# Finer loads of the first batch, a third input buffer and a reordered start in a Fourier-mixing and channel-mix kernel

## The chip, the cores and the metric

The kernel runs on one core of one Trainium2 chip. The metric is the device time of one execution in microseconds (us), and the number given is the median of ten executions.

A core has five engines that run their own instruction streams. The profile calls them PE (TensorE, matrix products), DVE (VectorE), ACT (ScalarE), POOL (GpSimd) and SP (SyncE, which here only issues transfers). PEld is the loading of a matrix into PE. Transfers between the chip's main memory (HBM) and the core's own memory (SBUF) are done by 16 DMA engines. They are issued from a queue of POOL, SP or ACT, and tell by a semaphore when they have landed. Matrix products go to a small memory called PSUM, from where ACT or DVE must "evacuate" them to SBUF.

## The reference

`x` has 8 batches of 3,072 rows of 256 numbers. First comes a two-dimensional Fourier transform of each batch, of which the real part is kept. Then comes a channel mix with a gate:

```python
X = np.fft.fft(np.fft.fft(x, axis=1), axis=2).real

x_prev = X shifted down by one row, zeros in the first row
xk = mu_k * X + (1.0 - mu_k) * x_prev
xr = mu_r * X + (1.0 - mu_r) * x_prev
k = np.maximum(xk @ w_k, 0.0)              # 256 -> 1024
v = k * k @ w_v                            # 1024 -> 256
out = v / (1.0 + np.exp(-(xr @ w_r)))      # w_r: 256 -> 256
```

## The kernel before

**The transform as matrix products.** The 3,072 rows are split into 96 partitions of 32 rows each. Stage A multiplies by a small matrix over the 96 partitions (`w_pm`), stage D transforms along the 256 columns (`w_eo`), and stage C finishes the transform along the rows with `m1` and `m2`, which hold sines of a table of angles. DVE then forms sums, differences (`halves`, `diff`) and the mixed inputs (`mix_part`, `mix`) for the channel mix.

**The channel mix.** For each of 48 chunks of 512 rows, four steps (`k_piece`) make the 1,024 hidden channels (L589), evacuated by ACT with Relu (L599); DVE squares them (L606), PE multiplies by `wv_sb` (L627), and DVE multiplies by the gate and writes the output tile (L637), which SP sends to memory. The transform of later batches is threaded between these steps by hand: `at(step, f, ...)` lists what is done at which step. At the end `pin_order` fixes the order of the instructions on each engine to the one in which they were written.

**Loads of x.** The loads convert from 32-bit to 16-bit numbers and are issued from POOL by `load_part(b, h, q0, nq)` (L102): half `h` (16 rows for each partition) of batch `b`, `nq` rows from `q0`. A half lives in a tile of the pool `xh`, which has two buffers (L58). The loads that concern us are:

- batch 0, half 0, in two parts of eight rows (L167, L172), and half 1 in four parts of four rows (L184 to L190);
- batch 1, half 0, in two parts of eight rows, and half 1 in one piece, in `loads()` (L372), between the weights: gathers of `wk` and `wr` by row numbers that POOL computes just before (`rows`, L287), and `wv`;
- later halves by `load_xh` (L107) at steps of the loop. A load into a buffer waits until the readers of the half that it held are done. For batch 0 and one half of batch 1 the reader is PE (`a_sum`, L444); for the others it is DVE (`butterfly`, L113), which writes even and odd sums that `a_item` then uses.

**The start.** Between the loads of batch 0, POOL makes counters with IOTA (`pcol_i`, `k1c_i`, `veo_i`, `kst_i`) and two small tables (`pd_f`, `ueo`). After the last load it makes `unit`, a 2 x 2 unit matrix (L191), with which `mu_turn` (L158) turns the rows of `mu_k` and `mu_r` into columns on PE. DVE and ACT make `w_pm`, `w_eo` and the angle tables meanwhile. `keep_busy` (L136) issues PE work on zeros.

**Stage A of batch 0.** `a_sum(b, h, q0, eng, n)` makes the products of `n` rows and evacuates them on the engine named (`"A"` for ACT, `"V"` for DVE). With `n` = 4 it takes one of three PSUM slots in turn (`ps_w`), with `n` = 2 one of two (`ps_v`). The order from L649 on is the one that the change edits. Into it are put the sine of the first 17 slices of angles (`m_sine(0, NS1)`, on ACT, NS1 = 17), `m_swap`, `m_zero`, and the second angles, slices 17 to 27, in two pieces (`m_angles(NS1, 22)` and `m_angles(22, NSL)`, on DVE, NSL = 27). After it come `mu_turn`, stage D in halves (`d_half`), stage C (`c_item`), and the first hidden products.

Of the kernel before, what the change touches and what calls it, by code (L numbers as in the profile page):

```python
# [13 lines left out]
AF = mybir.ActivationFunctionType  # L14
ALU = mybir.AluOpType
# [5 lines left out]
def _v(ap, extra_offset, free_dims):  # L21
    new_ap = [list(ap.ap[0])] + [[s, c] for (s, c) in free_dims]
    return dataclasses.replace(ap, offset=ap.offset + extra_offset, ap=new_ap)
# [12 lines left out]
def kernel(  # L36
# [10 lines left out]
    nc = tc.nc  # L47
# [5 lines left out]
    NSL = 27  # L53
    GU = 386
    NS1 = 17

    const = ctx.enter_context(tc.tile_pool(name="const", bufs=1))
    xh_pool = ctx.enter_context(tc.tile_pool(name="xh", bufs=2))  # L58
    eo_pool = ctx.enter_context(tc.tile_pool(name="eo", bufs=2))
    y_pool = ctx.enter_context(tc.tile_pool(name="y_sb", bufs=1))  # L60
    mix_pool = ctx.enter_context(tc.tile_pool(name="mix", bufs=1))
# [12 lines left out]
    def ps_w():  # L74
        return ps_slot("W", 3, 1024)

    def ps_v():
        return ps_slot("V", 2, 512)
# [23 lines left out]
    def load_part(b, h, q0, nq):  # L102

        nc.gpsimd.dma_start(out=xh_t[b, h][:, q0:q0 + nq],  # L104
                            in_=x_r[b, :, 16 * h + q0:16 * h + q0 + nq, :])
# [5 lines left out]
    V = nc.vector  # L111
# [24 lines left out]
    def keep_busy(n):  # L136

        ps = ps_v()
        for _ in range(n):
            nc.tensor.matmul(out=ps[:, 0:512], lhsT=zeros, rhs=_v(zeros, 0, [(0, 4), (1, P)]),  # L140
                             start=True, stop=True)
# [6 lines left out]
    unit = const.tile([2, 2], FP32)  # L148
# [3 lines left out]
    def mu_rows(a):  # L152
        for p0, f0, step, n in (((0, 0, 1, 1), (1, 1, 2, 64), (65, 2, 2, 63)),
                                ((0, 128, 1, 1), (1, 255, -2, 64), (65, 254, -2, 63)))[a]:
            nc.scalar.activation(out=mu_p[:, a, p0:p0 + n], in_=_v(mu_row, f0, [(step, n)]),
                                 func=AF.Copy)
# [7 lines left out]

    for h in range(2):
        xh_t[0, h] = xh_pool.tile([96, 16, 256], FP16, name="xh")
    load_part(0, 0, 0, 8)  # L167
    pcol_i = const.tile([P, 1], INT32)
    nc.gpsimd.iota(pcol_i, pattern=[[0, 1]], base=0, channel_multiplier=1)
    k1c_i = const.tile([P, 24, 2], INT32)  # L170
    nc.gpsimd.iota(k1c_i, pattern=[[1, 24], [0, 2]], base=0, channel_multiplier=0)
    load_part(0, 0, 8, 8)  # L172
    veo_i = const.tile([P, 2, 64], INT32)
    nc.gpsimd.iota(veo_i, pattern=[[-1, 2], [2, 64]], base=2, channel_multiplier=0)

# [4 lines left out]
                            op0=ALU.mult)  # L180
    for c in range(2):
        nc.gpsimd.tensor_scalar(out=ueo[:, :, c], in0=veo_i, scalar1=pd_f,
                                scalar2=(0.5 + 0.25 * c) * TURN, op0=ALU.mult, op1=ALU.add)
    load_part(0, 1, 0, 4)  # L184
    load_part(0, 1, 4, 4)
    kst_i = const.tile([P, NSL + 64], INT32)
    nc.gpsimd.iota(kst_i[:, 0:NSL], pattern=[[1, NSL]], base=-1, channel_multiplier=0)
    nc.gpsimd.iota(kst_i[:, NSL:NSL + 64], pattern=[[1, 64]], base=0, channel_multiplier=0)
    load_part(0, 1, 8, 4)
    load_part(0, 1, 12, 4)  # L190
    for i in range(2):  # L191
        nc.gpsimd.tensor_scalar(out=unit[:, i:i + 1], in0=pcol_i[0:2], scalar1=float(i),
                                scalar2=None, op0=ALU.is_equal)

    m_pi = const.tile([P, 1], FP32)
    V.memset(m_pi, -math.pi)
# [3 lines left out]
    def phase(lo, hi):  # L200
        lo, hi = (lo + 0.5) % 1.0, (hi + 0.5) % 1.0
        if (lo, hi) not in phs:
            t = const.tile([P, 1], FP32, name=f"ph{len(phs)}")
            V.memset(t[0:64], lo * TURN)
            V.memset(t[64:128], hi * TURN)
            phs[lo, hi] = t
        return phs[lo, hi]
# [12 lines left out]
    for c0, c1 in ((258, GU), (257, 258), (0, 1)):  # L220
        nc.scalar.activation(out=g_all[:, 13:NU, c0:c1],
                             in_=_v(zeros, 0, [(0, NU - 13), (1, c1 - c0)]), func=AF.Copy)
    mu_rows(0)

    pcol_f = const.tile([P, 1], FP32)
# [17 lines left out]
                    op0=ALU.mult, op1=ALU.add)  # L243
# [3 lines left out]
                    scalar2=0.5 / N1, op0=ALU.mult, op1=ALU.mult)  # L247
    V.tensor_tensor(out=u48, in0=u48, in1=ph48.rearrange("p a b -> p (a b)"), op=ALU.add)
    V.tensor_scalar(out=r48, in0=u48, scalar1=MAGIC, scalar2=MAGIC,
                    op0=ALU.add, op1=ALU.subtract)  # L250
    V.tensor_tensor(out=u48, in0=u48, in1=r48, op=ALU.subtract)
    nc.scalar.activation(out=t48, in_=u48, func=AF.Sin, bias=0.0, scale=TWO_PI)
    mu_rows(1)

    for g in range(2):
        for n in range(2):
            V.tensor_scalar(out=w_sg[:, n, g:g + 1], in0=g_i, scalar1=2.0 * g - 1.0,
                            scalar2=1.0 - g, op0=ALU.mult, op1=ALU.add)
        V.tensor_scalar(out=w_sg[:, 2, g:g + 1], in0=g_i, scalar1=1.0 - 2.0 * g,
                        scalar2=g - 1.0, op0=ALU.mult, op1=ALU.add)  # L260
# [5 lines left out]
                    op0=ALU.bitwise_and, op1=ALU.logical_shift_right)  # L266
# [4 lines left out]
                    op0=ALU.bitwise_and, op1=ALU.logical_shift_left)  # L271
# [7 lines left out]
                    scalar2=float(TURN) / R, op0=ALU.mult, op1=ALU.mult)  # L279
# [3 lines left out]
                    scalar2=phase(0.25, 0.0), op0=ALU.mult, op1=ALU.add)  # L283
# [33 lines left out]
    def m_angles(s0, s1):  # L317
        V.tensor_tensor(out=ang[:, s0:s1], in0=_v(ast, s0, [(1, s1 - s0), (0, 64)]),
                        in1=_v(ast, NSL, [(0, s1 - s0), (1, 64)]), op=ALU.add)
# [5 lines left out]
    def m_sine(s0, s1):  # L325
        nc.scalar.activation(out=m1[:, s0:s1], in_=ang[:, s0:s1], func=AF.Sin, bias=m_pi,
                             scale=TWO_PI / TURN)
# [3 lines left out]
    def m_swap(s0, s1):  # L331

        V.tensor_scalar(out=m2[lo64, s0:s1], in0=m1[hi64, s0:s1], scalar1=-1.0, scalar2=None,
                        op0=ALU.mult)
        V.tensor_copy(out=m2[hi64, s0:s1], in_=m1[lo64, s0:s1])
        if s0 == 0:
            for m in (m1, m2):
                V.memset(m[:, 0, 0:1], 0.0)

    def m_ends():  # L340


        for m in (m1, m2):
            nc.scalar.activation(out=m[hi64, 0], in_=m[hi64, 0], func=AF.Copy, scale=-1.0)

    def m_zero():
        for n, m in enumerate((m1, m2)):
            nc.scalar.activation(out=mz[lo64, n], in_=m[lo64, 1], func=AF.Copy)
# [73 lines left out]
    def evac(out_ap, in_ap, eng):  # L422
        if eng == "V":
            V.tensor_copy(out=out_ap, in_=in_ap)  # L424
        else:
            nc.scalar.activation(out=out_ap, in_=in_ap, func=AF.Copy)  # L426

    def a_tile(b):
        a_t[b] = y_pool.tile([P, 2, 48, 64], FP16, name="a")
# [13 lines left out]
    def a_sum(b, h, q0, eng="A", n=4):  # L443


        if (h, q0) == (0, 0):
            a_tile(b)
        xh = xh_t[b, h]
        ps = ps_w() if n == 4 else ps_v()
        for i in range(n):  # L450
            for k in range(2):
                nc.tensor.matmul(out=ps[:, 256 * i:256 * i + 192],  # L452
                                 lhsT=xh[:, q0 + i, 128 * k:128 * k + 128],
                                 rhs=w_pm[0:96, k:k + 2], start=(k == 0), stop=(k == 1))
        evac(_v(a_t[b], 2 * (16 * h + q0), [(64, 96), (2, n), (1, 2)]),
             _v(ps, 0, [(2, 96), (256, n), (1, 2)]), eng)
# [195 lines left out]
    a_sum(0, 0, 0)  # L652
    a_sum(0, 0, 4)
    keep_busy(1)
    m_sine(0, NS1)
    a_sum(0, 0, 8, "V")
    a_sum(0, 0, 12)
    m_angles(NS1, 22)
    m_swap(0, NS1)
    a_sum(0, 1, 0, "V")  # L660
    a_sum(0, 1, 4)
    m_zero()
    a_sum(0, 1, 8)
    a_sum(0, 1, 12, "V", 2)
    a_sum(0, 1, 14, "A", 2)
    m_angles(22, NSL)
    m_ends()
    mu_turn()
    d_half(0, 0, ps_v(), "A")
# [172 lines left out]
```

## Time and profile before

| what | us |
|---|---|
| median of ten executions | 455.89 (455.17 to 459.57) |
| the profiled execution | 456.39 |
| its span, first to last instruction | 454.6 |
| PE busy | 444.4 (98%) |
| ACT busy | 361.7 (80%) |
| DVE busy | 356.1 (78%) |
| POOL busy | 37.7 (8%) |

The span is what one execution's trace covers; some 1.8 us of the profiled execution lie around it. "Busy" sums the instructions of an engine. An engine may be busy all the time in one stage and idle in another, so the stages are looked at one by one. POOL works almost only in the first 45 us. Its transfers of x are these (issuing engine, number, size of each in 32-bit bytes, and the median time from issue to landing):

```profile
xh<-in_x_dram POOLq DMA_DIRECT2D x13, 768.0 KB, 6.9
xh<-in_x_dram POOLq DMA_DIRECT2D x4, 384.0 KB, 6.7
xh<-in_x_dram POOLq DMA_DIRECT2D x4, 192.0 KB, 6.3
```

The order of POOL's work at the start, with the start and the length of each group in us, is:

```profile
1.26 0.66 POOL L104 DMA_DIRECT2D xh<-in_x_dram  x1 [0.81 <-POOLq L826]
2.02 0.16 POOL L169 IOTA pcol_i<- 128x1 int32 x1
2.12 0.27 POOL L171 IOTA k1c_i<- 128x48 int32 x1
2.32 0.56 POOL L104 DMA_DIRECT2D xh<-in_x_dram  x1
2.88 0.27 POOL L174 IOTA veo_i<- 128x128 int32 x1
3.23 0.24 POOL L179 TENSOR_SCALAR pd_f<-pcol_i 128x1 f32<-128x1 int32 x1
3.57 0.77 POOL L182 TENSOR_SCALAR ueo<-veo_i,pd_f 128x128 int32<-128x128 int32 x2
4.30 1.06 POOL L104 DMA_DIRECT2D xh<-in_x_dram  x2
5.36 0.19 POOL L187 IOTA kst_i<- 128x27 int32 x1
5.47 0.22 POOL L188 IOTA kst_i<- 128x64 int32 x1
5.60 1.03 POOL L104 DMA_DIRECT2D xh<-in_x_dram  x2
6.64 1.40 POOL L192 TENSOR_SCALAR unit<-pcol_i 2x1 f32<-2x1 int32 x2
10.88 0.56 POOL L104 DMA_DIRECT2D xh<-in_x_dram  x1 [2.85 <-PE psW L452]
```

The bracket at the end of a line gives idle time of the engine before it and what ended it. The load at 10.88 is the first one of batch 1.

### The profile page before, as it was taken

The page shows a single profiled execution, that of the slowest core. Times are in us where ns is not written, and L with a number is a line of the kernel's source. Part 1 is how long each engine was busy: PE and PEld are TensorE (multiplying, and loading weights), DVE is VectorE, ACT ScalarE, POOL GpSimd, SP SyncE. Part 2 cuts the span into 40 slices and gives each one's busy share as a digit, 9 for nine tenths or more (in the row PEclk, how much of TensorE's full clock was granted, in tenths as well). Part 3 has the DMA queues.
Part 4 walks back from the last instruction along what each step waited for, and adds up shares of the span by engine and source line. Part 5 has one row for each costly group of instructions (what it writes and reads, how often), then busy time and mean ns, then how long its engine had stood idle before and what let it go on. Part 6 is the DMA issues. An engine that isn't in the chain of part 4 may idle for free.

```text
span 454.6 us, 9755 instructions
## 1 busy us (share of the span) xinstructions
PE 444.4 (98%) x4082; PEld 326.6 (72%) x4082; DVE 356.1 (78%) x495; ACT 361.7 (80%) x413; POOL 37.7 (8%) x72
## 2 busy tenths in 40 slices
PE   7899999999999999999999999999999999999995
PEld 4667777777777777777777777777777777666764
DVE  7899879977797869877789877987779755997453
ACT  7899997888788888788877888788878888666661
POOL 6848000000000000000000000000000000000000
PEclk9999999999999999999999999999999999999999
DMA  7775862627422473226622256221222122222223
GB/s 137 117 142 94 186 140 48 139 54 147 104 71 49 92 159 75 52 67 125 130 58 61 70 118 135 52 71 48 71 48 71 48 69 49 70 70 71 71 69 94
DMA packets 32524, 40.25 MB, mean 89 GB/s; under 512 B 3838, under 2 KB 29952, under 8 KB 31232
## 3 DMA queue, kind: packets, MB, share of 16 engines
q1 hardware_dynamic: 27776, 25.07, 22.0%
q0 software_dynamic: 4544, 14.42, 18.6%
q8 instruction: 32, 0.52, 0.5%
q10 hardware_dynamic: 160, 0.13, 0.1%
q14 instruction: 12, 0.10, 0.1%
HBM read 28.84 MB, written 25.17 MB: 119 GB/s over the span
## 4 chain that ended last, share of the span: by engine, by line
PE 93%; ACT 3%; DMA 1%; POOL 1%; issue 1%; DVE 0%; POOLq 0%
PE psV L627 37%; PE psW L589 35%; PE psW L613 9%; PE psW L462 4%; PE psW L438 4%; PE psW L493 3%; DMA xh<-in_x_dram 1%; ACT rl L599 1%; ACT g_all L426 1%; POOL xh L104 1%; PE psW L452 0%; DVE g_all L424 0%; ACT L618 0%; ACT pq L426 0%; ACT r L618 0%
## 5 line engine op out<-in xcount | busy, mean ns | idle before, releaser
L599 ACT ACTIVATE rl<-psW 128x1024 f16<-128x1024 f32 x192 | 196.2, 1025 | 79.6 <-PE psW L589 79.4
L627 PE MATMUL psV<-wv_sb,k 128*128 128x256 f16 x1536 | 198.6, 272 | 0.0
L589 PE MATMUL psW<-x,wk 128*128 128x512 f16 (+1 forms) x776 | 196.6, 377 | 0.3 <-ACT rl L599 0.3
L606 DVE TENSOR_TENSOR k<-rl 128x2048 f16<-128x2048 f16 (+1 forms) x98 | 117.5, 1202 | 61.3 <-ACT rl L599 60.6
L627 PEld LDWEIGHTS <-k 128*128 128x128 f16 x1536 | 143.7, 98 | 20.1
L589 PEld LDWEIGHTS <-wk 128*128 128x128 f16 x776 | 75.8, 98 | 50.2 <-issue 0.4
L637 DVE SCALAR_TENSOR_TENSOR o<-psV,r 128x512 f32<-128x512 f32 (+1 forms) x97 | 66.2, 684 | 23.3 <-PE psV L627 21.3
L558 DVE TENSOR_TENSOR x<-y,t 128x1536 f16<-128x1536 f16 x60 | 57.5, 959 | 2.1
L426 ACT ACTIVATE a<-psW 128x768 f16<-128x768 f32 x61 | 49.0, 808 | 1.6 <-PE psW L452 1.6
L613 PE MATMUL psW<-wr,x 128*128 128x256 f16 x384 | 49.8, 273 | 0.0
L618 ACT ACTIVATE r<-psW 128x1024 f16<-128x1024 f32 x48 | 49.0, 1020 | 0.8 <-PE psW L613 0.8
L613 PEld LDWEIGHTS <-x 128*128 128x128 f16 x384 | 37.6, 98 | 14.4
L426 ACT ACTIVATE g_all<-psW 128x1024 f16<-128x1024 f32 (+1 forms) x47 | 47.9, 1027 | 0.0
L117 DVE TENSOR_TENSOR eo<-xh 96x2048 f16<-96x2048 f16 x26 | 31.5, 1214 | 1.6 <-DMA xh<-in_x_dram 1.6
L462 PEld LDWEIGHTS <-a 128*128 128x128 f16 x384 | 25.0, 98 | 10.1 <-issue 0.6
L438 PEld LDWEIGHTS <-eo 96*128 96x128 f16 x416 | 23.4, 97 | 11.6
L104 POOL DMA_DIRECT2D xh<-in_x_dram x21 | 11.2, 538 | 225.5 <-DVE eo L117 221.7
L426 ACT ACTIVATE pq<-psW 128x896 f16<-128x896 f32 (+5 forms) x34 | 28.9, 851 | 0.8 <-PE psW L462 0.4
L462 PE MATMUL psW<-w_eo,a 128*128 128x128 f16 x376 | 28.3, 219 | 0.3 <-ACT rl L599 0.3
L438 PE MATMUL psW<-w_pm,eo 96*128 96x96 f16 x416 | 26.3, 205 | 0.0
L493 PEld LDWEIGHTS <-g_all 128*128 128x128 f16 x459 | 17.8, 98 | 8.8 <-ACT g_all L426 1.7
L493 PE MATMUL psW<-m,g_all 128*128 128x64 f16 x442 | 19.2, 193 | 1.4 <-ACT g_all L426 0.8
(107 smaller groups left out, 168.3 us busy)
## 6 DMA issues: line engine op xcount, KB each, us to landing
out_dram<-o SPq DMA_DIRECT2D x190, 128.0 KB, 2.4
xh<-in_x_dram POOLq DMA_DIRECT2D x13, 768.0 KB, 6.9
xh<-in_x_dram POOLq DMA_DIRECT2D x4, 384.0 KB, 6.7
xh<-in_x_dram POOLq DMA_DIRECT2D x4, 192.0 KB, 6.3
wv_sb<-in_moe_w_v_dram POOLq DMA_DIRECT2D x1, 512.0 KB, 8.5
out_dram<-o ACTq DMA_DIRECT2D x2, 64.0 KB, 2.0
out_dram<-o SPq DMA_DIRECT2D x2, 64.0 KB
y<-f SPq DMA_DIRECT2D x7, 3.4 KB
```

The costliest lines, as they stand in the source:

```text
L426: nc.scalar.activation(out=out_ap, in_=in_ap, func=AF.Copy)
L438: nc.tensor.matmul(out=ps[:, 128 * i:128 * i + 96], lhsT=eo[:, 8 * j + i, e, :], rhs=w_pm[0:96, 0], start=True, stop=True)
L462: nc.tensor.matmul(out=_v(ps, 256 * i + 64 * (1 - e), [(128, 2), (1, 64)]), lhsT=a_t[b][:, e, 2 * u:2 * u + 2, :], rhs=w_eo[:, e, :], star ...
L493: nc.tensor.matmul(out=ps[:, o + 64 * i:o + 64 * i + 64], lhsT=g_all[:, u, col:col + 128], rhs=m[:, sl] if sl != 1 else mz[:, 0 if m is m1 ...
L558: V.tensor_tensor(out=dst, in0=_v(y_t[b], 64 * (NSL * a + lo + 3 * m), [(1, n)]), in1=_v(x_t["t", a], 64 * lo, [(1, n)]), op=ALU.subtract ...
L589: nc.tensor.matmul(out=st["k", ds][:, 512 * hs + lo:512 * hs + hi], lhsT=wk_sb[m][a][:, 128 * fc:128 * fc + 128], rhs=xk[:, a, 512 * i + l ...
L599: nc.scalar.activation(out=st["rl"][:, 2 * ds:2 * ds + 2], in_=st["k", ds].rearrange("p (f t) -> p f t", f=2), func=AF.Relu, bias=0.0, sca ...
L606: V.tensor_tensor(out=k2_t[c][:, lo:hi], in0=r, in1=r, op=ALU.mult)
L613: nc.tensor.matmul(out=ps[:, 256 * tb:256 * tb + 256], lhsT=x_t[b, 1, m][:, a, 512 * i + 128 * tb: 512 * i + 128 * tb + 128], rhs=wr_sb[m] ...
L618: nc.scalar.activation(out=st["r", c], in_=ps, func=AF.Sigmoid)
L627: nc.tensor.matmul(out=st["v", tb - h][:, 256 * h:256 * h + 256], lhsT=k2_t[c][:, fc, 128 * tb:128 * tb + 128], rhs=wv_sb[:, fc], start=(f ...
L637: V.scalar_tensor_tensor(out=o.rearrange("p a b -> p (a b)")[:, 0:256 * n], in0=st["v", t0][:, 0:256 * n], scalar=16.0, in1=st["r", c][:, ...
```

## The change

The pool `xh` gets three buffers. Half 0 of batch 0 is loaded in four parts of four rows, so that all of batch 0 comes in eight parts; the IOTAs and tables of POOL stand at other places between the loads. `unit` is made by ACT, from `pcol_f`, a copy of the partition numbers. In stage A the third group of rows (0, 8) is evacuated by ACT, ahead of the sine, and the engines of the next ones alternate accordingly. The second angles are made in one piece, at the place of the second of the two.

```diff
-    xh_pool = ctx.enter_context(tc.tile_pool(name="xh", bufs=2))
+    xh_pool = ctx.enter_context(tc.tile_pool(name="xh", bufs=3))
...
-    load_part(0, 0, 0, 8)
+    load_part(0, 0, 0, 4)
     pcol_i = const.tile([P, 1], INT32)
     nc.gpsimd.iota(pcol_i, pattern=[[0, 1]], base=0, channel_multiplier=1)
     k1c_i = const.tile([P, 24, 2], INT32)
     nc.gpsimd.iota(k1c_i, pattern=[[1, 24], [0, 2]], base=0, channel_multiplier=0)
-    load_part(0, 0, 8, 8)
+    load_part(0, 0, 4, 4)
+    load_part(0, 0, 8, 4)
     veo_i = const.tile([P, 2, 64], INT32)
     nc.gpsimd.iota(veo_i, pattern=[[-1, 2], [2, 64]], base=2, channel_multiplier=0)
...
-    load_part(0, 1, 0, 4)
-    load_part(0, 1, 4, 4)
+    load_part(0, 0, 12, 4)
     kst_i = const.tile([P, NSL + 64], INT32)
     nc.gpsimd.iota(kst_i[:, 0:NSL], pattern=[[1, NSL]], base=-1, channel_multiplier=0)
     nc.gpsimd.iota(kst_i[:, NSL:NSL + 64], pattern=[[1, 64]], base=0, channel_multiplier=0)
-    load_part(0, 1, 8, 4)
-    load_part(0, 1, 12, 4)
-    for i in range(2):
-        nc.gpsimd.tensor_scalar(out=unit[:, i:i + 1], in0=pcol_i[0:2], scalar1=float(i),
-                                scalar2=None, op0=ALU.is_equal)
+    for q0 in range(0, 16, 4):
+        load_part(0, 1, q0, 4)
...
     mu_rows(1)
+
+    for i in range(2):
+        nc.scalar.activation(out=unit[:, i:i + 1], in_=pcol_f[0:2], func=AF.Copy,
+                             bias=1.0 - i, scale=2.0 * i - 1.0)
...
     a_sum(0, 0, 0)
     a_sum(0, 0, 4)
     keep_busy(1)
+    a_sum(0, 0, 8)
     m_sine(0, NS1)
-    a_sum(0, 0, 8, "V")
-    a_sum(0, 0, 12)
-    m_angles(NS1, 22)
+    a_sum(0, 0, 12, "V")
     m_swap(0, NS1)
-    a_sum(0, 1, 0, "V")
-    a_sum(0, 1, 4)
+    a_sum(0, 1, 0)
     m_zero()
+    a_sum(0, 1, 4, "V")
     a_sum(0, 1, 8)
     a_sum(0, 1, 12, "V", 2)
     a_sum(0, 1, 14, "A", 2)
-    m_angles(22, NSL)
+    m_angles(NS1, NSL)
     m_ends()
     mu_turn()
```

## The prediction

> **What bounds it.** I read the page first, part 4 (the chain that ended last) and part 1.
>
> ```profile
> PE 93%; ACT 3%; DMA 1%; POOL 1%; issue 1%; DVE 0%; POOLq 0%
> ```
>
> TensorE is the bound for the whole; the rest of the chain is small, so the question is where it lies. The diff touches the start (and, by the third buffer, x loads later), so next I took the chain of waits in order of time.
>
> ```profile
> 4.34 1.02 POOL xh L104 x2
> 5.37 0.18 POOL kst_i L187
> 5.54 0.14 POOL kst_i L188
> 5.69 0.41 POOL xh L104
> 6.10 6.78 DMA xh<-in_x_dram
> 12.88 0.05 issue
> 12.93 0.83 PE psV L452 x8
> 13.76 0.55 PE psW L161 x4
> ```
>
> Each line is start, length, what. The first 12.88 us are set by x of batch 0: the last part, issued at 6.10, lands at 12.88, and then stage A, `mu_turn`, stage D and stage C follow one another with no slack down to the first products at about 20. After 34.7 us PE is busy 415.07 of 419.90 us in a table by stage. A shift of the last landing therefore goes through one to one. Was that landing bound by issue or by transfer? The windows view (length, five engines, clock, DMA share, GB/s written):
>
> ```profile
> 4.00:6.75 2.75, 2.08 (x16) 1.24 (x15) 2.44 (x18) 1.75 (x9) 2.75 (x8) 1.00 1.01 203
> 7.25:11.00 3.75, 2.15 (x26) 1.92 (x24) 2.57 (x5) 2.49 (x4) 0.90 (x2) 1.00 1.08 186
> 11.25:12.00 0.75, 0.66 (x9) 0.43 (x7) 0.69 (x3) 0.24 (x2) 0.57 (x3) 1.00 0.16 27
> ```
>
> The DMA share is full from 4 to 11: bound by transfer. The first row holds the eight-row parts (4,096 B written per partition), the second the four-row parts (2,048 B), which run slower, 186 against 203 GB/s. The third shows a tail: nearly all engines are done, and the last part still has not landed.
>
> The largest wait on x in the table of waits is this one:
>
> ```profile
> POOL xh L104 <- DVE eo L117: 221.7, 10, 44.4
> ...
> DVE eo L117 <- DMA xh<-in_x_dram: 1.6, 1, 1.6
> ```
>
> It looks like what a third buffer removes, but it is POOL, with nothing else to do, waiting to refill early; DVE waits for x once, 1.6 us at 51, and no PE wait follows it there.
>
> **The skill.** "DMA: Bandwidth & Descriptors", section on the anatomy of a DMA from GpSimd, gives about 2 us fixed plus bytes over a rate, most of the fixed part being the receipt. Here a part took 4.5 to 10.9 us from issue to landing because they queue behind each other; queued, only the rate counts, and I use the trace's. The same page, section on latency, says that two of the sixteen engines, 7 and 15, are usually slower for such DMAs, with descriptor fetches as a guess at the cause; the third window row agrees in kind (engines aren't named in it). "SBUF — State Buffer", section on who interferes with whom: a DVE instruction with two SBUF inputs holds up a GpSimd one that reads SBUF, and one in a two-port mode blocks GpSimd wholly. The trace agrees: of the two `unit` instructions on POOL one took 1.196 us, beside DVE's L318 (6.68 to 7.97), the other 0.215. "TensorE: Matmul & The Clock Gate", section "Part 1": the array runs at half clock until some 3.4 us of work, and falls back after an idle window. Here `keep_busy` matmuls start 0.43 us apart up to 5 us, while the two at 17.4 need 0.59 together and one takes 0.38, so 0.21 apart: agrees.
>
> **Part by part.** The sum is made against the profiled execution, 456.39 us, of which the span is 454.6; it lies 0.5 above the median 455.89.
>
> *x in eight parts.* An eight-row part writes 96 x 4,096 = 393,216 B: 1.94 us at 203 GB/s. Two four-row parts of 196,608 B at 186: 2 x 1.06 = 2.11. The change splits two such parts: 2 x 0.18 = +0.35 us of transfer ahead of the last byte. Bounds: 0, if the rate is set by something else, and +0.8, if the slow engine of the tail pays more for each packet than the mean (its lag is about 1.4 us: the bulk ends at 11.25, the trace's last packet of the load at 12.6; it carried a sixteenth, 12 large and 24 small data packets, and 12 more at 1.4/36 each add 0.47). I take 0.35.
>
> *Are they issued in time?* An issue costs POOL 0.53 us, and the first bytes move about 1.25 us after its start (1.26 to 2.5). POOL's new row: parts 1 to 3 at 1.26, 2.32, 2.85; `veo_i`, `pd_f`, `ueo` end at 4.87 in place of 4.34; part 4 at 4.83; `kst_i` at 5.36 as before (two issues ahead of it either way); parts 5 to 8 at 5.60, 6.13, 6.66, 7.19. With data from 2.5, about 0.5 us of slow start and 1.06 each, parts 1 to 3 are through at 6.2; part 4 is visible at 6.08. Part 8 is visible at 8.4 and wanted at 10.4. No hole; at most 0.1.
>
> *ueo later by 0.53.* DVE reads it at 4.90, so DVE slips by up to 0.1, then `w_eo` on ACT; the Sin of the first angles starts at 8.77 and its result is wanted by the swap and by stage C at 15.4. Hidden; 0.1 if not.
>
> *unit on ACT.* Two tiny activations, by the three of `mu_rows` in 0.48, 0.16 each. They fall into this gap:
>
> ```profile
> 4.29 0.48 ACT L155 ACTIVATE mu_p<-mu_row 2x1 f32<-2x1 f32 x3
> 5.22 0.51 ACT L391 ACTIVATE w_eo<-ueo,m_pi 128x256 f16<-128x256 int32 x1 [0.45 <-DVE ueo L269]
> ```
>
> 4.77 + 0.32 = 5.09: free. `pcol_f` is there since 2.4. POOL loses 1.40 us after its last x issue, also free of charge, for the matmuls that use `unit` run at 13.69.
>
> *Third stage A evacuation.* Three and a half evacuations stay on ACT and two and a half on DVE; only their order changes (0.81 on ACT, 0.96 on DVE). Rows 8 to 11 land at about 7 (6.3 for the bulk, some lag), so ACT evacuates them at about 7.8 to 8.6, just ahead of the Sin. If late by 1 us, the Sin ends at 11 and the swap at 12, still ahead of the last part. DVE's fourth comes at about 9 in place of 12's at 9.96. The end of stage A waits for the last part in both.
>
> *Angles in one piece.* Two of 0.48 become one of 640 elements: 0.14 + 640 x 1.06 ns = 0.82 (from 0.48 at 320 and 1.29 at 1,088). It starts at about 13.94 + 0.35; the copy of `mu_f` ends at 15.25, DVE's stage D evacuation is due at 15.35. Hidden by 0.1 us; 0.1 to 0.2 if not. The gain, 0.48 earlier on DVE, lay beside the wait for x.
>
> *Third buffer.* POOL no longer waits until 10.88 for stage A to free x(0,0): the first half of x(1,0) is issued at about 7.7, and the gathers of wk, then wv and wr follow some 3 us earlier. Two more DMAs shift POOL's eight reused semaphores by two; the second wk gather then waits for the third part of x, long landed. Who waits for the weights? In the trace of before PE and ACT have no wait on wk, wv or wr: the first product starts behind stage C at 20.1, and ACT is busy almost without a hole from 20.3 to 31. So 0. These transfers queue behind x of batch 0, hence no harm to it. Later loads run up to 12 us (one of 57 moves to about 46) or a batch ahead, at a DMA share of 0.38: nothing waits for them, 0.
>
> Sum: +0.35. Span 454.95, profiled 456.74, median 456.2.
>
> **Rivals.** *A shorter tail.* Finer parts, or a POOL not blocked by `unit`, could let the lagging engine keep up: its whole lag is 1.4, less 0.35: median 454.9. For it: the tail; against: a slow engine gets more packets, not fewer.
>
> *Descriptors starved.* The last three issues now lie at 6.13 to 7.7, beside DVE's L318 (two SBUF inputs) and just ahead of L322 (8.00 to 8.73, one input, 1,088 elements in 0.73, faster than one a cycle in L318). If POOL can't finish part 7 until 8.73, its bytes start near 10.0 instead of 9.3, and part 8's follow: about +0.7, with the 0.35 to median 456.9. Against: writing descriptors isn't reading, and issues at 10.88 and 17.92 beside DVE work took 0.56 and 0.61.
>
> *PE's clock.* The slow side. Stage A in eight evenly spaced bursts of 0.75 in 1.06 us could leave an activity window too empty, so that PE falls to half clock from about 13 to 20, where it lies on the chain: 0.83 + 0.55 + 0.64 + 0.35 + 0.56 + 0.54 + 0.54 = 4.0 us; less 7 x 0.2 of fill, 2.6 doubles. Median 455.89 + 0.35 + 2.6 = 458.8. It decides once the array is idle for a whole window. Against: before has one hole of 1.6 us (7.5 to 9.08) and stayed fast; the new holes are 0.3.
>
> *Doing nothing it says.* If something I call free, an evacuation or the gathers, is what the chain waits for, either sign to about 1 us.
>
> **Numbers.** A measurement of this kernel tells about 0.5% (2.3 us) from no change. Forecast, 0 to +0.8: 0.53. Shorter tail 0.15, starved 0.14, clock or another slow mechanism of that size 0.11, the last 0.07 (half of it each way). Only the clock case passes +2.3, and some of the unknown: slower 0.14; faster needs more than the whole tail: 0.06; same 0.80. Range: from the short tail, 454.8, to beyond the starved case with the spread of the runs, 457.7.
>
> **What would show it.** Right: in the chain, the DMA of x ends at 13.1 to 13.4, no hole in the DMA share from 4 to 11, the first x(1,0) issue near 7.7, `unit` on ACT before 5.2, the first product at 20.4, no new PE wait. Wrong: landing before 12.5 (shorter tail), a DMA share under 0.8 around 9 to 10 (starved), stage D or C matmuls lengthened (clock), or a time outside 453.6 to 458.2, which would mean a place after 20 us that I take for idle is not.

## The result and the profile after

| | before | after |
|---|---|---|
| median | 456.1 (51 executions) | 460.07 (14 executions) |
| lowest, highest | 455.14, 461.17 | 458.5, 460.75 |
| the profiled execution | 456.39 | 460.02 |
| its span | 454.6 | 458.2 |
| its mean granted clock of TensorE | 1.000 | 0.989 |

All times are in us. The ratio is 1.0068, with a 95% interval of 1.0047 to 1.0088: the change makes the kernel slower, by 3.1 us by the ratio and 4.0 by the medians, where +0.3 was forecast. Executions of one kernel differ in their mean granted clock: of the 171 executions of before that ran beside the experiments (one of 781.68 us left out), 28 lie below 0.9965 with a median of 457.6, the rest at 455.75, so a median here is over a mixture, and "the clock held" below means 0.9965 or more.

First part 2 of the two pages, 40 slices of some 11.5 us each: the row of granted clocks, before and after.

```profile
PEclk9999999999999999999999999999999999999999
PEclk9599999999999999999999999999999999999999
```

The second slice, 11.5 to 23 us, is at half clock. Nothing else in the row changed, so what the clock costs, it costs there. Next the chain of waits of after (start, length, what), over the same stretch as the one shown of before:

```profile
5.84 5.25 DMA xh<-in_x_dram
11.09 0.05 issue
11.13 3.88 PE psW L453 x24
15.01 1.28 PE psV L453 x8
16.29 0.94 PE psW L161 x4
17.23 0.97 PE psV L463 x8
18.20 0.85 PE psW L463 x8
```

Of before, the chain had only the last part of x and then 0.83 for eight stage A products. Now PE itself is late: from 11.13 it works without a pause. Eight stage A products of the last part take 1.28 in place of 0.83, the turn of the mu rows 0.94 in place of 0.55, and stage D's first eight 0.97 in place of 0.64.

The last part of x landed at 14.11, by the last of its semaphore updates that the trace has (fifteen of sixteen), where it had landed at 12.88: 1.23 later. From that landing to the first hidden product (L590, at 23.75; before at 20.14) it is 9.64 in place of 7.26: 2.38 more. The two make 3.61, and the spans differ by 3.6. After 24 us nothing is lost or won.

The windows of after, the same three as of before and one more (length; busy time and count of PE, PEld, DVE, ACT and POOL; clock, DMA share, GB/s):

```profile
4.00:6.75 2.75, 2.02 (x15) 1.16 (x14) 2.29 (x17) 2.13 (x11) 2.65 (x7) 1.00 0.94 145
7.25:11.00 3.75, 1.96 (x19) 1.22 (x16) 2.21 (x4) 2.71 (x3) 2.82 (x8) 1.00 0.95 132
11.25:12.00 0.75, 0.75 (x7) 0.72 (x6) 0.71 (x2) 0.00 (x0) 0.73 (x2) 0.60 0.97 169
14.00:21.00 7.00, 7.00 (x69) 6.59 (x67) 4.34 (x9) 4.02 (x8) 5.94 (x8) 0.50 1.08 168
```

The DMA engines are nearly as occupied as before (0.94 and 0.95, before 1.01 and 1.08), but write 145 and 132 GB/s in place of 203 and 186. So for the most part it is not a hole between issues: some packets take longer. Of the packets of 2,048 B that start between 9 and 10 us the middle one took 173 ns in both kernels, but the mean was 317 in place of 206, and the longest took 1.79 us in place of 0.63. PE meanwhile had thin work. Its timeline of after (start, length, what; the bracket is idle time before it and what ended it):

```profile
6.80 0.58 PE L453 MATMUL psW<-w_pm,xh 96*128 96x192 f16 x5
7.21 0.38 PE L140 MATMUL psV<-zeros 128*128 128x512 f16 x1
7.54 0.83 PE L453 MATMUL psW<-w_pm,xh 96*128 96x192 f16 x8
9.68 0.83 PE L453 MATMUL psW<-w_pm,xh 96*128 96x192 f16 x8 [1.30 <-DMA xh<-in_x_dram]
11.13 2.12 PE L453 MATMUL psW<-w_pm,xh 96*128 96x192 f16 x13 [0.62 <-DMA xh<-in_x_dram]
```

The clock of 0.60 over the last 0.75 us before 12 puts its fall at 11.4; it is 0.50 until 21 and 0.68 from 21 to 22, so it stays halved until about 21.6, although PE is busy all the time from 11.13 (by the profile, which models the ends of products).

The clock records of all eighteen traces, of before, after and the experiments below, show more. Inside a trace the clock changes only at whole multiples of 3.41 us, counted from the moment when it first is full, and that moment lies anywhere between 3.9 and 6.3 us. In after, the step that ended with the fall is this one, with 1.49 us of work:

```profile
7.99:11.40 3.41, 1.49 (x17) 1.04 (x15) 1.87 (x4) 2.13 (x3) 2.48 (x6) 1.00 0.94 123
```

In nine of the ten traces whose clock fell early, PE was busy for 0.68 to 1.79 us in the step before the fall (in e13, the tenth, for 2.46); in no step of any trace behind which a full clock held was it busy for less than 2.14. The clock then stayed halved for one step (e13), two (e11, e12, e15, e16), three (after, e2, e4, e7) or four (e6).

The thinnest 3.41 us of before hold 1.7 us of work in its profile. So how the steps happen to lie may decide whether an execution falls. That is inferred, since one execution of each kernel was traced; and e10, with no less than 2.35 in its profile, lost clock in nine of 19 executions.

The other edits show in the timelines of POOL and ACT of after. POOL, from `ueo` to the last issues of x at the start:

```profile
4.09 1.00 POOL L183 TENSOR_SCALAR ueo<-veo_i,pd_f 128x128 int32<-128x128 int32 x2
...
5.84 2.55 POOL L104 DMA_DIRECT2D xh<-in_x_dram  x5
```

The last line holds half 1's four parts and, at 7.85, the first part of batch 1, which had waited until 10.88. ACT:

```profile
4.64 0.28 ACT L253 ACTIVATE unit<-pcol_f 2x1 f32<-2x1 f32 x2
5.47 0.51 ACT L392 ACTIVATE w_eo<-ueo,m_pi 128x256 f16<-128x256 int32 x1 [0.56 <-DVE ueo L270]
```

`unit` lies in ACT's gap. On DVE the second angles in one piece start at 16.16 and take the 0.82 worked out. The table of waits still has POOL's long wait for buffers (before 221.7) and DVE's one wait for x:

```profile
POOL xh L104 <- DVE eo L117: 212.6, 9, 44.4
...
DVE eo L117 <- DMA xh<-in_x_dram: 1.5, 1, 1.5
```

### The profile page after: what moved, and what is told of

It is laid out like the page before. It is cut to its first block, busy times and chain, and to the rows that moved or that the text cites. A ratio compares the mean times of both kernels' runs of the same rounds, so it can differ in the third digit from the quotient of the medians.

```text
span 458.2 us, 9755 instructions
## 1 busy us (share of the span) xinstructions
PE 448.7 (98%) x4082; PEld 330.8 (72%) x4082; DVE 356.2 (78%) x494; ACT 362.2 (79%) x415; POOL 38.4 (8%) x72
## 4 chain that ended last, share of the span: by engine, by line
PE 94%; ACT 2%; DMA 1%; POOL 1%; issue 0%; DVE 0%; POOLq 0%
PE psV L628 36%; PE psW L590 35%; PE psW L614 9%; PE psW L463 4%; PE psW L439 4%; PE psW L494 3%; PE psW L453 1%; DMA xh<-in_x_dram 1%; ACT rl L600 1%; ACT g_all L427 1%; POOL xh L104 0%; PE psV L453 0%; POOL ueo L183 0%; PE psV L463 0%; PE psW L161 0%
## 5 line engine op out<-in xcount | busy, mean ns | idle before, releaser
L590 PE MATMUL psW<-x,wk 128*128 128x512 f16 (+1 forms) x776 | 196.6, 377 | 0.3 <-ACT rl L600 0.3
L590 PEld LDWEIGHTS <-wk 128*128 128x128 f16 x776 | 75.8, 98 | 50.2 <-issue 0.7
L463 PEld LDWEIGHTS <-a 128*128 128x128 f16 x384 | 26.4, 102 | 9.9 <-issue 0.4
L104 POOL DMA_DIRECT2D xh<-in_x_dram x23 | 12.2, 539 | 213.5 <-DVE eo L117 212.6
L463 PE MATMUL psW<-w_eo,a 128*128 128x128 f16 x376 | 29.4, 224 | 0.3 <-ACT rl L600 0.3
```

Of the source, the lines that this page charges most:

```text
L463: nc.tensor.matmul(out=_v(ps, 256 * i + 64 * (1 - e), [(128, 2), (1, 64)]), lhsT=a_t[b][:, e, 2 * u:2 * u + 2, :], rhs=w_eo[:, e, :], star ...
L590: nc.tensor.matmul(out=st["k", ds][:, 512 * hs + lo:512 * hs + hi], lhsT=wk_sb[m][a][:, 128 * fc:128 * fc + 128], rhs=xk[:, a, 512 * i + l ...
```

## The experiments

Each was run beside the kernel before on the same chip, and a ratio is to that kernel. A diff is against the kernel named ahead of it. "Landing" is the last semaphore of x of batch 0.

**Keep PE's clock (e1), and the third buffer alone (e2, e3).** e1 is after with more work on zeros between the bursts; e2 is after with two buffers; e3 is before with three.

```diff
     a_sum(0, 0, 8)
+    keep_busy(3)
     m_sine(0, NS1)
     a_sum(0, 0, 12, "V")
+    keep_busy(3)
     m_swap(0, NS1)
     a_sum(0, 1, 0)
+    keep_busy(3)
     m_zero()
     a_sum(0, 1, 4, "V")
+    keep_busy(2)
```

> The changed kernel with more work on zeros for PE inside stage A of batch 0: keep_busy(3) after rows 8 and after rows 12 of half 0 and after rows 0 of half 1, keep_busy(2) after rows 4. Theory clock (the thin stage A lets PE fall to half clock from 11.3 to 21.3 us, and that is most of the loss): the granted clock stays at 1.00 in every slice, the time falls by 2 us or more, to 457.0 to 458.0; what is left over the kernel before, about 1.2, is the later landing of x (14.11 against 12.88). Theory landing (the late x alone, the clock is a symptom that costs little): within 0.7 of the changed kernel, 459.4 to 460.7.

```diff
-    xh_pool = ctx.enter_context(tc.tile_pool(name="xh", bufs=3))
+    xh_pool = ctx.enter_context(tc.tile_pool(name="xh", bufs=2))
```

> The changed kernel with two buffers for x again, so that POOL waits for stage A before it issues the first load of batch 1 and works out row numbers. Theory third buffer (POOL's next load, its row arithmetic and the gathers, all pulled forward to 7.85 to 11 us, slow the descriptors or packets of batch 0's last parts): packets of 1.3 to 1.8 us vanish, x lands at about 13.0, the clock mostly holds, time 456.0 to 457.2. Theory finer parts (more and smaller packets are what is slow): the landing stays near 14, time 459.0 to 460.5.

The reverse of that line, in before:

> The kernel before with the third buffer alone. Theory third buffer: x of batch 0 lands 0.5 to 1.2 us later than 12.88 and the time is 457 to 459.5. Theory finer parts: landing at 12.9, time 455.7 to 456.5.

e1: 458.94 against 456.31, ratio 1.0056 [1.0037, 1.0075]. In its windows the clock stays:

```profile
7.25:11.00 3.75, 3.39 (x27) 1.87 (x24) 2.56 (x4) 2.71 (x3) 2.82 (x8) 1.00 1.05 155
11.25:12.00 0.75, 0.74 (x9) 0.74 (x10) 0.72 (x2) 0.00 (x0) 0.73 (x2) 1.00 1.07 161
12.00:21.00 9.00, 7.54 (x100) 5.75 (x98) 5.75 (x15) 6.16 (x13) 7.21 (x12) 1.00 1.08 174
```

From landing (14.28) to stage D (15.79) it takes 1.51, as in before (12.88 to 14.34, 1.46), where after took 3.12. So the half clock is real and removable, but the transfer is about as slow as in after, and of the 4.0 us between the medians 1.1 came back (1.6 of 3.6 between the spans). One of the 16 executions of after with a clock on record held it, and took 459.17, which fits. The rest is the landing, 1.4 later than in before, and some 0.6 more up to the first hidden product (22.17 in place of 20.14): the first evacuation of `pq` starts only at 18.51, its products done at 17.54, and for that I have no cause.

e2: 460.0, ratio 1.0066 [1.0043, 1.0089]. e3: 455.51, ratio 0.9997 [0.9975, 1.002]. Taking the third buffer away does not help after (landing 14.90), and adding it does not hurt before: it is not the cause. Among the executions that held the clock, e3 is even the faster one, 455.47 (11) in place of 456.18 (15).

**The eight parts alone (e4), and everything but them (e5).** e4 is before with after's eight loads at their places on POOL (the `load_part` lines of the diff in the section on the change); all else is as before. e5 is after with the six loads where they were:

```diff
-    load_part(0, 0, 0, 4)
+    load_part(0, 0, 0, 8)
...
-    load_part(0, 0, 4, 4)
-    load_part(0, 0, 8, 4)
+    load_part(0, 0, 8, 8)
...
-    load_part(0, 0, 12, 4)
+    load_part(0, 1, 0, 4)
+    load_part(0, 1, 4, 4)
...
-    for q0 in range(0, 16, 4):
-        load_part(0, 1, q0, 4)
+    load_part(0, 1, 8, 4)
+    load_part(0, 1, 12, 4)
```

> The kernel before with the loads of batch 0 in eight parts and POOL's order of the changed kernel, two buffers, unit still on POOL and the old order of evacuations. Theory finer parts: landing near 14, the clock falls in most runs, 458.5 to 460.5. Theory third buffer: only the 0.35 of smaller packets, 456.0 to 457.0.

> The changed kernel with the loads of batch 0 in six parts at the old places (two of eight rows, four of four), everything else as changed: third buffer, unit on ACT, the new order of evacuations, the second angles in one piece. If the parts are the whole loss: x lands at 12.0 to 12.9, granted clock 0.997 or more in most runs, time 455.2 to 456.3. If the other edits cost too (the third evacuation ahead of the sine on ACT now waits for rows 8 to 15, landing at 8.1 to 9.1, so the sine and the swap come about 1.5 us later): 456.5 to 457.5.

e4: 460.34 against 456.31, ratio 1.0088 [1.0066, 1.011], clock 0.986 to 0.993. e5: 455.12 against 455.97, ratio 0.9984 [0.9971, 0.9997]. So the eight parts, with their places on POOL, make the whole loss, and the rest of the change together is a small gain here that they covered. The chain of e5:

```profile
6.10 5.85 DMA xh<-in_x_dram
11.94 0.05 issue
11.99 0.83 PE psV L453 x8
```

and its windows:

```profile
4.00:6.00 2.00, 1.64 (x6) 0.45 (x5) 1.76 (x14) 1.65 (x10) 2.00 (x6) 1.00 1.03 205
6.00:8.00 2.00, 2.00 (x22) 1.69 (x21) 1.89 (x5) 1.31 (x3) 1.92 (x4) 1.00 1.05 200
8.00:10.00 2.00, 2.00 (x26) 1.91 (x25) 1.61 (x3) 1.87 (x3) 1.43 (x5) 1.00 1.06 175
```

Nearly the same POOL, ACT and DVE work, full rate, clock 1.00. Its first packet of a four-row part starts at 6.78, so that the window from 6 to 8 is mixed; e10, below, tells of four-row parts alone.

**Which of the parts? (e6, e10, e11)** e6 loads half 1 in two parts of eight rows; e10 and e11 load half 0 as 8, 4, 4 and as 4, 4, 8 rows. All are edits of after.

```diff
# e6
-    for q0 in range(0, 16, 4):
-        load_part(0, 1, q0, 4)
+    for q0 in range(0, 16, 8):
+        load_part(0, 1, q0, 8)
# e10
-    load_part(0, 0, 0, 4)
+    load_part(0, 0, 0, 8)
...
-    load_part(0, 0, 4, 4)
# e11
-    load_part(0, 0, 8, 4)
+    load_part(0, 0, 8, 8)
...
-    load_part(0, 0, 12, 4)
```

> The changed kernel with half 1 of batch 0 in two parts of eight rows; half 0 stays in four of four. Theory late descriptors (an engine runs dry because POOL issues the later parts at 5.84 to 7.85, too close to when they are wanted and beside DVE's angles): the issues end by 6.9, the hole from 8 to 10 us goes, GB/s there at 170 or more, landing at 12.9 or earlier though half 0 stays fine, time 456.0 to 457.5. Theory small parts (each part of four rows is slow as such): about half of the loss is left, landing at 13.3 or later, 457.5 to 459.

> The changed kernel with seven parts: the first of eight rows, then two of four for the rest of half 0, half 1 in four of four. Theory start (four-row parts are slow only when they are the first, while the engines are still getting under way): about 200 GB/s from 4 to 6 us, landing at 12.0 to 12.9, time 455.2 to 456.5. Theory any small part before 6 us: loss of half or more of the changed kernel's, landing at 13 or later, 457.5 or more.

> The changed kernel with seven parts: two of four rows first, then one of eight, issued at 2.88, half 1 in four of four. Theory start: 135 to 150 GB/s from 4 to 6 us, the engines stay out of step, landing at 13.3 to 14.5, time 458 to 460.5. Theory number of parts (each part above six costs the same): half of the loss, about 457.5, as in the other order with seven parts.

e6: 460.91, 1.0087 [1.0062, 1.0111], landing 14.25. e11: 457.86, 1.005 [1.0034, 1.0067], landing 13.61. e10: 456.4, 1.0038 [1.002, 1.0057], but with another picture: its profiled execution has span 453.7 and landing 12.54, and in the windows

```profile
4.00:6.00 2.00, 1.45 (x4) 0.27 (x2) 1.85 (x15) 1.65 (x9) 2.00 (x6) 1.00 1.04 200
6.00:8.00 2.00, 1.93 (x21) 1.80 (x22) 1.90 (x5) 1.16 (x3) 1.88 (x5) 1.00 1.10 203
```

Ten of its 19 executions held the clock, with a median of 456.06, and nine did not, with 458.97. Its packets of four-row parts start at 5.09, so the second window has no others: behind a head of eight, parts of four rows can run at full rate (from 8 to 10 us they have 173, much as in before, 173, and e5, 175). Parts of four rows are not slow as such. Most of what e10 loses, it loses by the clock, about 2.9 us when it falls; the ten executions that held it are still 0.7 above those of before beside them that did (455.38), and the cause of that is open.

**Late issues (e7), packets (e12), a lead (e13, e14).** Why is a small head slow? e7 issues all eight parts of after in a row, with POOL's counters and tables behind them (issues from 2.32 to 5.90 without a gap). e12 splits half 0 by partitions instead of rows, so that the four parts have the same bytes as in after but packets of 4,096 B. e13 is after with the second part issued right behind the first, at 1.91. e14 is e5 with its second part issued late, at 3.69.

```diff
# e7
     load_part(0, 0, 8, 4)
+    load_part(0, 0, 12, 4)
+    for q0 in range(0, 16, 4):
+        load_part(0, 1, q0, 4)
# e12
+    def load_rows(b, h, q0, nq, p0, p1):
+        nc.gpsimd.dma_start(out=xh_t[b, h][p0:p1, q0:q0 + nq],
+                            in_=x_r[b, p0:p1, 16 * h + q0:16 * h + q0 + nq, :])
...
-    load_part(0, 0, 0, 4)
+    load_rows(0, 0, 0, 8, 0, 48)
...
-    load_part(0, 0, 4, 4)
-    load_part(0, 0, 8, 4)
+    load_rows(0, 0, 0, 8, 48, 96)
+    load_rows(0, 0, 8, 8, 0, 48)
...
-    load_part(0, 0, 12, 4)
+    load_rows(0, 0, 8, 8, 48, 96)
# e13: load_part(0, 0, 4, 4) moved ahead of pcol_i
# e14: load_part(0, 0, 8, 8) moved behind ueo
```

> The changed kernel with all eight issues of batch 0 ahead of veo_i, pd_f, ueo and kst_i (the last issue at about 5.6 instead of 7.35). Its angles and w_eo come 2 to 3 us later, so the time may not fall; the landing is what tells. Theory late descriptors: GB/s of 180 or more from 4 to 10 us and landing at 12.0 to 12.7. Theory small parts: 135 to 170 GB/s as in the changed kernel and landing at 13.8 or later.

> The changed kernel with half 0 in four parts again, but each of eight rows of 48 partitions: as many parts, issues and semaphores as changed, with packets of 4,096 B as before. Theory packet size (the short packets are what is slow): 195 to 205 GB/s from 4 to 6 us, landing at 12.0 to 13.0, 455.2 to 456.7. Theory number of parts and their issues (descriptor sets, semaphore writes, POOL's timing): 135 to 160 GB/s, landing at 13.5 or later, 458.5 to 460.5.

> The changed kernel with the second part of batch 0 issued directly after the first, ahead of pcol_i and k1c_i (start at about 1.92 instead of 2.32); the two counters and w_pm come 0.5 later. Theory lead (an engine that comes to the end of the small first part before the second part's descriptors are there loses its step): 180 GB/s or more from 4 to 6 us, the sixteen landings of the second part within 0.7 us of each other instead of 1.2, the last landing at 12.3 to 13.2, time 455.5 to 457.5. Theory small first part as such: nothing moves, 135 to 145 GB/s, landing at 14 or later, 459 to 460.5.

> The fast version (changed kernel, six parts) with its second part of eight rows issued after ueo, at about 3.8 instead of 2.32, so that it is visible only at about the time the first is through (5.0 to 5.2). Theory lead: the engines lose step with parts of eight rows too, packets of over 0.5 us from 5 to 9, landing at 13.3 or later, 457 to 460. Theory small first part as such: a hole of at most 0.4 us around 5.2, landing at 12.0 to 12.9, 455.1 to 456.3.

| | ratio | landing | GB/s at 4-6, 6-8, 8-10, 10-12 us |
|---|---|---|---|
| after | 1.0068 [1.0047, 1.0088] | 14.11 | 135, 170, 126, 135 |
| e7 | 1.0023 [1.0009, 1.0038] | 13.61 | 139, 133, 174, 197 |
| e12 | 1.0065 [1.0044, 1.0086] | 14.69 | 148, 142, 148, 125 |
| e13 | 1.0069 [1.0049, 1.0088] | 14.61 | 179, 131, 161, 153 |
| e14 | 0.9988 [0.9978, 0.9997] | 12.00 | 156, 196, 205, 218 |

e7 recovers its rate after 8 us and 0.5 us of the landing, so issue times matter a little; but with every descriptor there early the stretch from 4 to 8 is as slow as in after. Thirteen of its 22 executions held the clock (median 456.58), nine did not (458.82): again the clock is worth over 2 us in one and the same kernel. Larger packets change nothing (e12). An early second part lifts the first window and lowers the next, and the landing is no earlier (e13). A late second part leaves a hole at 5 us, after which the rate is full (e14). Late issue, packet size and lead are out as the main cause.

**One small part at the head (e15, e16).** e5 with its first two parts of 4 and 12, or 6 and 10 rows, issued at the same times:

```diff
# e15; e16 with 6 and (6, 10)
-    load_part(0, 0, 0, 8)
+    load_part(0, 0, 0, 4)
...
-    load_part(0, 0, 8, 8)
+    load_part(0, 0, 4, 12)
```

> The fast version (changed kernel, six parts) with its first two parts of four and twelve rows instead of eight and eight: six parts, six issues at the same places, only the first part is small. Theory small first part as such: one is enough, under 165 GB/s over 4 to 8 us, landing at 13.3 or later, 457 to 460. Theory several small parts early: it takes more than one, landing at 12.0 to 12.9; stage A of rows 4 to 15 then starts late, at about 8.2, 455.3 to 457.

> The same with six and ten rows. Theory small first part as such, with a bound between four and eight rows: landing between that of 4 and 12 (13.3 or later if slow) and that of 8 and 8 (11.94). Theory several small parts early: landing at 12.0 to 12.9, 455.2 to 456.5.

e15: 459.57 against 455.79, ratio 1.007 [1.0049, 1.0091], landing 14.23. Only the border between the first two parts differs from e5:

```profile
4.00:6.00 2.00, 2.00 (x12) 1.14 (x10) 1.76 (x14) 1.64 (x10) 2.00 (x6) 1.00 0.78 123
6.00:8.00 2.00, 0.21 (x3) 0.00 (x0) 1.89 (x4) 1.01 (x2) 1.92 (x4) 1.00 0.86 150
8.00:10.00 2.00, 0.20 (x2) 0.20 (x3) 0.80 (x2) 0.00 (x0) 1.43 (x5) 0.74 0.98 159
```

205, 200 and 175 GB/s have become 123, 150 and 159. (The clock falls here for a further reason: the coarse second part leaves PE without rows for 3.59 us.) e16: 456.35, ratio 1.0011 [0.9988, 1.0035], between the two in time: ten of 20 executions held the clock at a median of 455.2, ten had 458.85. Its profiled one is of the latter, with 202 GB/s from 4 to 6 and then 156, and its landing is not between the two as expected, but at 14.34, later than in e15: fifteen of the sixteen engines were done by 13.01, one came 1.33 behind them. How a head of six rows behaves stays open.

Over all kernels: ten whose first part holds 196,608 B (after, e1, e2, e4, e6, e7, e11, e12, e13, e15) land x between 13.61 and 14.93 or later, seven whose first part holds 393,216 B (before, e3, e5, e8, e9, e10, e14) between 11.9 and 13.13. These are single profiles; the pair that differs in nothing else is e5 and e15.

**Fill the hole of before (e8), and of e5 (e9).** e8 is before with three buffers and `keep_busy(4)` in place of `keep_busy(1)` after rows 4 to 7. e9 is e5 with the same and `keep_busy(2)` after rows 12 to 15.

```diff
     a_sum(0, 0, 4)
-    keep_busy(1)
+    keep_busy(4)
```

> The kernel before with the third buffer and keep_busy(4) instead of keep_busy(1) after rows 4 to 7 of stage A. If the slow executions of the kernel before (457 to 459.5, with a granted clock of 0.991 to 0.995) come from PE's idle hole between 7.5 and 9.08 us: no execution under 0.997, none above 457, median 455.3 to 455.8. If they come from elsewhere: the same spread as before, a fifth to a quarter of the executions above 457.

> The changed kernel with the loads of batch 0 in six parts at the old places, and more work on zeros: keep_busy(4) instead of keep_busy(1) after rows 4 to 7, keep_busy(2) after rows 12 to 15. If the two gains add (six parts with the rest of the change 455.12; the fill, which took the slow executions out of the kernel before): 454.7 to 455.1, no execution with a clock under 0.997. If the clock was already held by the new order: 455.0 to 455.4, no gain over six parts alone.

e8: 455.03 against 455.97, ratio 0.9975 [0.996, 0.9989]; all 22 executions held the clock, between 454.58 and 456.58, where 8 of the 51 of before beside them did not. The third buffer alone (e3) lost some clock in three of 14. The timeline of PE of before has the hole of 1.60:

```profile
7.11 0.38 PE L140 MATMUL psV<-zeros 128*128 128x512 f16 x1
9.08 3.16 PE L452 MATMUL psW<-w_pm,xh 96*128 96x192 f16 x33 [1.60 <-DMA xh<-in_x_dram]
```

That of e8 shows the fill, 1.03 in place of 0.38, and a hole of 1.41 left:

```profile
7.08 1.03 PE L140 MATMUL psV<-zeros 128*128 128x512 f16 x4
9.51 2.73 PE L452 MATMUL psW<-w_pm,xh 96*128 96x192 f16 x31 [1.41 <-DMA xh<-in_x_dram]
```

The thinnest 3.41 us hold 2.0 us of work in e8's profile, where they held 1.7. But the clock is not most of e8's gain: among executions that held it, e8 is still 0.87 faster than before (455.03 against 455.90), about as much as e3. So the third buffer may carry much of it; how the gain divides is not shown.

e9: 455.17, ratio 0.9998 [0.9985, 1.0011]: no gain from more fill shows, e5's clock holds without it in 13 of 14 executions. e8 and e5 beat the kernel before beside which they ran, by 0.25% and 0.16%, and after, and can't be told apart. But e9, which is e5 with more fill, did not beat the before beside it, which ran on another chip and lost clock in one of 33 executions. So the gain of e5 over before is not settled.

## Why the prediction was wrong

**Eight parts, "2 x 0.18 = +0.35": this step failed.** It took 186 GB/s, measured from 7.25 to 11 us for four-row parts in the middle of a stream, as the rate of four-row parts, and put it at the head. As a rate behind an eight-row head it was fair: such parts run at 173 to 205 (e10 from 6 to 10 us, e14 from 8 to 10). To carry it to the head was wrong: a first part of 196,608 B brings the following transfers down to 123 to 159 GB/s from 4 to 6 us (179 in e13, with the fall to 131 just after), in parts of four, eight or twelve rows. The landing came 1.23 later, above the bound of +0.8 as well. Why a small head does this is not shown: packet size, late descriptors and lead are excluded as the main cause, and no kernel here looked into the order in which the engines did their work.

**"No hole; at most 0.1"** was nearly right in its words and misled: the DMA share was 0.94 and 0.95 over the two windows, with 0.75 from 10 to 11 us. A full share said that engines were occupied, not that bytes moved; the check I named for starved issues could not see this loss.

**PE's clock, the rival at 0.11, came true.** Its price, 2.6, was of the right size for this profile, 2.38, and for 2.2 to 3.6 between executions of the same kernel in e7, e10 and e16, whose landings may differ too. For the medians it was too high: e1, with the clock held, got back 1.1, and stayed 2.75 above the executions of before that held theirs. What misjudged its chance were two sentences. "The new holes are 0.3" followed from the +0.35: with the real transfer they were 1.30 and 0.62 us. And "before has one hole of 1.6 us" and "stayed fast" rested on one profiled execution; 28 of 171 executions of before lost some clock. "It decides once the array is idle for a whole window" was wrong too. The Trainium skill, "TensorE: Matmul & The Clock Gate", section "Why this matters for your kernels", advises against idle gaps over about 3 us; here no gap passed 1.30, and 1.49 us of work in 3.41 were too few. The section "Part 1: The HAM clock gate" of the same page has the full clock return after some 3.4 us of sustained work; this trace shows PE busy throughout from 11.13 and at half clock until 21.6, where e13 came back after 3.41. The measurements decide.

**The two losses are one chain.** The small head slows the transfer, the slower transfer thins PE's bursts, the clock falls, and the halved clock stretches stage A's end and what follows. e1 filled the bursts, held the clock and kept the first loss; e5 took the small head away and had neither.

**The steps costed at nothing held.** The third buffer: x of batch 1 issued at 7.85 (forecast 7.7), no loss that e2 or e3 can tell, and perhaps part of the gain (see e3 and e8). `ueo` later: it took 1.00 in place of 0.77, and `w_eo` slipped by 0.25 rather than 0.1, with nobody waiting. `unit` and the angles: as worked out; the order of evacuations costs nothing that shows. With the third buffer they gain 0.85 us in e5, by the medians, over the before beside it. How that gain divides is not shown; in e5's profile x landed at 11.94, without the one engine that in before finished 0.95 behind the other fifteen, and a single profile doesn't say whether the change did that.

**The rivals.** A shorter tail did not come: engines spread wider. Starved descriptors explain at most the 0.5 that e7 regains. That a time outside 453.6 to 458.2 "would mean a place after 20 us that I take for idle is not" was wrong as well: all of the loss had arisen by the first hidden product at 23.75, from the late landing and the halved clock.

## What to carry to other kernels

Price a finer load by what the head of its own stream does, not by a rate taken from the middle of another; try the size of the first part alone, since here it decided the landing by 2.3 us (e15 against e5). Where loads feed PE in bursts, count PE's work per step of the clock (here 3.41 us) and compare the clock of many executions, not of one: in e8, three more products on zeros at the thin place cost nothing that its time shows, and none of 22 executions lost clock. And split a bundle of edits before judging it, for here a gain of at most 0.2% lay under a loss of 0.9%.

## What the runs showed of the hardware that was not expected

- A first transfer of 196,608 B in place of 393,216 B lowered the rate of the next ones from about 200 to between 123 and 159 GB/s over 4 to 6 us (179 in e13), at a DMA share of 0.78 to 0.99 (1.03 in e13), with single packets of up to 1.79 us in after where 0.17 is usual. The cause is not known.
- The clock of PE changed only in steps of 3.41 us, whose place differs from execution to execution. It fell behind steps with 0.68 to 1.79 us of work (once 2.46) and held behind steps with 2.14 or more, though no gap in after passed 1.30; in after it came back only after 10.24 us, in all of which PE was busy.
- Of before, 28 of 171 executions lost some clock. With four products on zeros instead of one ahead of its hole of 1.60 us it was none of 22, beside eight of 51 of before (e8, which has a third buffer too): likely the fill, but 22 are few.
